# One region of 64x64 products per quad in a window-attention training kernel

## The chip, the cores and the metric

The kernel runs on one core of a Trainium2 chip. The metric is the device time of one execution in microseconds (us); the median of three timed runs stands below. A core has a matrix engine (TensorE, PE in the views; its weight loads are listed apart as PEld), a vector engine (VectorE, DVE), a scalar engine (ScalarE, ACT), GpSimd (POOL) and SyncE (SP), each with an instruction queue of its own that it works through in order, and 16 DMA engines that move data. SP and POOL issue this kernel's transfers. TensorE writes its results to PSUM, which has 8 banks; a bank holds 128 x 512 numbers in f32, and VectorE or ScalarE copy ("evict") results from there to SBUF.

## The reference

Attention inside windows of 8 x 8 pixels over a 256 x 256 image with 384 channels, one head, in bf16, and all its gradients:

```python
def forward(x, wqkv, wo):            # x: 1 x 256 x 256 x 384
    xw = windows(x)                  # 1024 windows of 64 pixels x 384
    qkv = xw @ wqkv
    q, k, v = qkv[..., :C], qkv[..., C:2 * C], qkv[..., 2 * C:]
    p = softmax(einsum('bqc,bkc->bqk', q, k) * C ** -0.5)
    return unwindows(einsum('bqk,bkc->bqc', p, v) @ wo)

out, vjp = jax.vjp(forward, x, wqkv, wo)
return (out, *vjp(grad_out))         # out, dx, dwqkv, dwo
```

## The kernel before

**Algebra.** The kernel multiplies the weights together once. With A = scale Wq Wk^T and B = Wv Wo, a window's scores are x A x^T, its output is P (x B), and the gradients need `y` (x with A), `z` (grad_out with B^T), `u` = x B and `v` (x with A^T). dS is the gradient of the scores. dx is the sum P^T z + dS^T y + dS v. The weight gradients come from two 384 x 384 sums over all pixels, x^T U and x^T W with U = dS x and W = P^T grad_out, kept in `GF_acc` and multiplied out at the end.

**Tiles.** Two windows lie on the 128 partitions, one on the lower 64 (`LO`), one on the upper (`HI`). Four such pairs make a quad; there are 128 quads. Everything that mixes channels is a full 128 x 128 product (`product`, L145). Everything inside one window is 64 x 64 and is done in `attend` (L249) by `slot`, which issues four 64 x 64 matmuls (L266) that occupy the four quarters of the array: two halves of a "straight" product and two of a "crossed" one. A call of `attend` treats two of the quad's four `t` and has six slots; a row of consecutive slots is called a region here.

**Pipeline.** `step(c, b, a, ahead)` works on three quads at once: attention of quad `c`, scores and softmax of `b`, projections of `a`, and loads for one three quads ahead. The schedule is by hand: on each engine instructions run in the order in which the Python code issues them. On TensorE one step is: `scores` of b (`sd`, 24 short products), eight `uv` evictions' products (`pj`, 384 wide), three groups of z products (`pj`, 512 wide), one group of 12 weight-gradient products (`filler(1)`, tile `pg`), the six slots of `attend(c, (0, 1))`, three groups of y products, another `pg` group, the six slots of `attend(c, (2, 3))`. A group of weight gradients sums over three quads (`GQ`), so 12 products go into one bank and VectorE adds the bank to `GF_acc` (L321).

**Evictions.** ScalarE evicts `uq` and `vq` (L235), z and y into `yz` (L159, L161), the outputs `o` (L270), most of the dx banks `pd` (L270, L296, half of the L297 copies) and one `Wq` of each pair (L281), and stacks `Pb` into `ps` (L211). VectorE evicts `Uq` (L285, L289), the other `Wq` (L283), the upper half of `pd[1]` of the first pair (L297), gathers `yz` into `zy` (L167) and does the softmax and its gradient (`soft`).

**Transfers.** SP's queue holds, in order, per step: the transposes `dT` and `xT` of a coming quad (L134), the transpose `PS<-ps` (L239), four loads of `xq` (L126), and the transpose `tok<-zy` (L171) that turns y and z. POOL's queue holds four loads of `dq` (L127) and nine output transfers (L298 to L305).

**PSUM.** All eight banks come from one pool, `ring`. A tile takes a bank when `ring.tile` is called for it, and its first write waits until the reader of the bank's tile before has finished. `attend` takes all its eight banks at its start:

```python
pw = {t: bank("pw") for t in pair}
pu = {t0: bank("pu")}
pd = [bank("pd") for outer in (0, 1)]
po = {t0: bank("po")}
pu[t1] = bank("pu")
po[t1] = bank("po")
```

The `pd` banks collect through the whole region; `pw`, `pu` and `po` are written by one slot each.

Of the kernel before, what the change touches and what calls it, by code (L numbers as in the profile page):

```python
# [9 lines left out]
ALU = mybir.AluOpType  # L10
# [12 lines left out]
def kernel(  # L23
# [91 lines left out]
    def windows(ap, st, first, count=2):  # L115
        row, col = st["at"]
        return ap[0, row + WIN * first:row + WIN * (first + count), col:col + WIN, :]
# [68 lines left out]
    def soft(st, step):  # L186
        sd = st["sd"]
        if step == 0:
            st["mx"] = mx = sm.tile([P, QUAD], F32, tag="mx", name="mx")
            for w, h in ((0, HI), (1, LO)):  # L190
                nc.vector.tensor_reduce(out=mx[h, :], in_=sd[h, :, w, :], axis=AX.X, op=ALU.max)
        elif step == 1:
            mx = st["mx"]
            st["sh"] = sh = sm.tile([P, QUAD, WT], F32, tag="sh", name="sh")
            for w, h, o in ((0, HI, LO), (1, LO, HI)):
                nc.vector.tensor_tensor(out=sh[o, :, :], in0=sd[h, :, w, :], in1=over_k(mx[h, :], WT),
                                        op=ALU.subtract)
        elif step == 2:
            st["ex"] = ex = sm.tile([P, QUAD, WT], F32, tag="ex", name="ex")
            nc.scalar.activation(out=ex[:], in_=st["sh"][:], func=ACT.Exp)  # L200
        elif step == 3:
            ex = st["ex"]
            rs = sm.tile([P, QUAD], F32, tag="rs")
            nc.vector.tensor_reduce(out=rs[:], in_=ex[:], axis=AX.X, op=ALU.add)
            ri = sm.tile([P, QUAD], F32, tag="ri")
            nc.vector.reciprocal(out=ri[:], in_=rs[:])
            st["Pb"] = Pb = qp.tile([P, QUAD, WT], BF16, tag="Pb", name="Pb")
            nc.vector.tensor_tensor(out=Pb[:], in0=ex[:], in1=over_k(ri[:]), op=ALU.mult)  # L208
            st["ps"] = ps = qp.tile([P, QUAD, 2, WT], BF16, tag="ps", name="ps")
            for w, h in ((0, LO), (1, HI)):  # L210
                nc.scalar.copy(out=ps[h, :, w, :], in_=Pb[h, :, :])  # L211
        elif step == 4:
            st["pr"] = pr = sm.tile([P, QUAD, WT], F32, tag="pr", name="pr")
            for w, h in ((0, LO), (1, HI)):
                nc.vector.tensor_tensor(out=pr[h, :, :], in0=sd[h, :, w, :], in1=st["Pb"][h, :, :], op=ALU.mult)
            st["D"] = D = sm.tile([P, QUAD], F32, tag="D", name="D")
            nc.vector.tensor_reduce(out=D[:], in_=pr[:], axis=AX.X, op=ALU.add)
        else:
            pd = sm.tile([P, QUAD, WT], F32, tag="pd")
            nc.vector.tensor_tensor(out=pd[:], in0=st["Pb"][:], in1=over_k(st["D"][:]), op=ALU.mult)  # L220
            ps = st["ps"]
            for w, h, o in ((0, LO, HI), (1, HI, LO)):
                nc.vector.tensor_tensor(out=ps[o, :, w, :], in0=st["pr"][h, :, :], in1=pd[h, :, :], op=ALU.subtract)
            st["dS"] = dS = qp.tile([P, QUAD, WT], BF16, tag="dS", name="dS")
            nc.vector.tensor_tensor(out=dS[:], in0=st["pr"][:], in1=pd[:], op=ALU.subtract)

    def uv(st, t, part):
        if t == 0 and part == 0:
# [20 lines left out]
    def attend(st, pair):  # L249
        if pair[0] == 0:  # L250
            st["Uq"] = grp.tile([P, QUAD, C], BF16, tag="Uq", name="Uq")
            st["Wq"] = grp.tile([P, QUAD, C], BF16, tag="Wq", name="Wq")

        def bank(name):
            return ring.tile([P, C], F32, tag="r", name=name)
# [12 lines left out]
        def keep(name, src):  # L268
            sb = ob.tile([P, C], BF16, tag=name, name=name)
            nc.scalar.copy(out=sb[:], in_=src[:])  # L270
            return sb

        t0, t1 = pair
        pw = {t: bank("pw") for t in pair}
        pu = {t0: bank("pu")}
        pd = [bank("pd") for outer in (0, 1)]
        po = {t0: bank("po")}
        pu[t1] = bank("pu")
        po[t1] = bank("po")
        slot((pw[t0], "Pb", "dq", t0), ("Pb", "z", t0), start=True)  # L280
        nc.scalar.copy(out=st["Wq"][:, t0, :], in_=pw[t0][:])  # L281
        slot((pw[t1], "Pb", "dq", t1), ("dS", "y", t0))
        nc.vector.tensor_copy(out=st["Wq"][:, t1, :], in_=pw[t1][:])  # L283
        slot((pu[t0], "ST", "xq", t0), ("Pb", "z", t1), start=True)
        nc.vector.tensor_copy(out=st["Uq"][:, t0, :], in_=pu[t0][:])  # L285
        slot((po[t0], "PT", "uq", t0), ("dS", "y", t1))
        o0 = keep("o", po[t0])
        slot((pu[t1], "ST", "xq", t1), ("ST", "vq", t0), stop=True)
        nc.vector.tensor_copy(out=st["Uq"][:, t1, :], in_=pu[t1][:])  # L289
        slot((po[t1], "PT", "uq", t1), ("ST", "vq", t1), stop=True)  # L290
        o1 = keep("o", po[t1])
        inner = keep("d", pd[0])
        if t0 == 0:
            st["mid"], st["rim"] = [ob.tile([P, C], BF16, tag="d", name="d") for k in range(2)]
# [6 lines left out]
        if t0 == 0:  # L301
            nc.gpsimd.dma_start(out=windows(out_1, st, 0, 1), in_=st["rim"][HI, :])
        else:
            nc.gpsimd.dma_start(out=windows(out_1, st, 3), in_=st["mid"][:])
            nc.gpsimd.dma_start(out=windows(out_1, st, 7, 1), in_=st["rim"][LO, :])  # L305

    fill = []

    final = {}

    def gf_group(sts, last=False):
        n = len(sts) * QUAD
        for f in range(2):
            if last:
                final[f] = grp.tile([P, CK, C], BF16, tag="Uq", name="GFb")
            for ma in range(CK):
                pw = ring.tile([P, C], F32, tag="r", name="pg")
                for i in range(n):
                    st, t = sts[i // QUAD], i % QUAD
                    product(pw[:], st["xq"][:, t, ma * P:(ma + 1) * P], st["UW"[f] + "q"][:, t, :], i == 0, i == n - 1)  # L320
                nc.vector.tensor_tensor(out=GF_acc[:, f, ma, :], in0=pw[:], in1=GF_acc[:, f, ma, :], op=ALU.add)  # L321
                if last:
                    nc.vector.tensor_copy(out=final[f][:, ma, :], in_=GF_acc[:, f, ma, :])
                yield

    def filler(n):
        while n and fill:
            try:
                next(fill[0])
                n -= 1  # L330
            except StopIteration:
                fill.pop(0)

    def step(c, b, a, ahead):


        def on(st):
            return (lambda f, *r: f(st, *r)) if st is not None else (lambda f, *r: None)
        C_, B, A = on(c), on(b), on(a)
        B(scores)  # L340
        B(soft, 0)
        if b is not None and c is None:
            weight_rest()
        B(uv, 0, 0)
        B(uv, 0, 1)
        B(soft, 1)
        B(uv, 1, 0)
        B(uv, 1, 1)
        B(soft, 2)
        B(soft, 3)  # L350
        B(uv, 2, 0)
        B(uv, 2, 1)
        B(uv, 3, 0)
        B(uv, 3, 1)
        B(soft, 4)
        for mo in range(CK):
            A(project, 0, mo)
        B(soft, 5)
        B(turn)
        if ahead is not None:  # L360
            load(ahead)
        filler(1)
        C_(attend, (0, 1))
        A(gather, 0)
        for mo in range(CK):
            A(project, 1, mo)
        A(gather, 1)
        A(to_tokens)
        filler(1)
        C_(attend, (2, 3))  # L370

    G_ON_PE, X_ON_PE = 4, 1
    EV = {"z": "AAA", "y": "AAA", "u": "AAAA", "v": "AAAA", "o": "AAAA", "U": "DDDD", "W": "DDDD", "d": "AAAA"}
    quads = [(row, col) for row in range(0, H, 2 * WIN * QUAD) for col in range(0, W, WIN)]
    sts = [{"at": q, "i": i} for i, q in enumerate(quads)]
    n = len(sts)
# [41 lines left out]
    with tc.manual_schedule(engines=MANUAL):  # L418
# [19 lines left out]
        for i in range(-1, n + 1):  # L438
            if 0 <= i < n - 2:
                load_turn(sts[i + 2])  # L440
            step(get(i - 1), get(i), get(i + 1), get(i + AHEAD) if i >= 0 else None)
            if 0 < i + 2 < G_ON_PE:
                turn_on_pe(sts[i + 2], "dq", "dT")
            if i == 1:
                turn_blocks(woT_sb, wo_sb)
            if i > 0:
                held.append(sts[i - 1])
                sts[i - 1] = None
            if held and i == n:
                last = gf_group(held, True)  # L450
            elif len(held) == GQ:
                fill.append(gf_group(held))
                held = []
        filler(1 << 30)
        weight_gradients(last)


# [28 lines left out]
```

## Time and profile before

| | |
|---|---|
| timed runs | 1947.11, 1947.42, 1947.66 us; median 1947.42 |
| the profiled execution | span 1942.8 us, 48771 instructions |
| granted TensorE clock | 0.999 |
| busy time in one quad (1009.30 to 1024.09, 14.79 us) | PE 14.79, PEld 8.29, DVE 11.24, ACT 11.96, POOL 6.96 us |
| full products, mean of one | `pg` and 384-wide `pj` 326 ns, 512-wide `pj` 381 ns |
| 64x64 products, mean of one | 323 to 335 ns |
| the adds to `GF_acc` (L321) | 258, mean 558 ns |
| TensorE's waits for DMA (PE rows) | `dT` 5.1 us in 4 waits, `PS` 1.5 us in 3 |
| DMA | 423.21 MB, mean 218 GB/s; the engines' mean busy share is 0.9 or more in nearly all of 40 slices |
| issue to landing, median | `tok` 7.6, `xT` 6.3, `dT` 5.9, `PS` 4.7 us |

The profiled execution is one run; its span leaves out about 4.6 us of what a timed run has. Matmuls are pipelined: a matmul's duration is its latency, and the distance between the starts of two neighbours is what it costs. A wait is shown as idle time before an instruction with what ended it. A bank tells nothing by itself in the profile; which reader frees which bank is read from the built program's order.

### The profile page before, as it was taken

The page shows a single profiled execution, that of the slowest core. Times are in us where ns is not written, and L with a number is a line of the kernel's source. Part 1 is how long each engine was busy: PE and PEld are TensorE (multiplying, and loading weights), DVE is VectorE, ACT ScalarE, POOL GpSimd, SP SyncE. Part 2 cuts the span into 40 slices and gives each one's busy share as a digit, 9 for nine tenths or more (in the row PEclk, how much of TensorE's full clock was granted, in tenths as well). Part 3 has the DMA queues.
Part 4 walks back from the last instruction along what each step waited for, and adds up shares of the span by engine and source line. Part 5 has one row for each costly group of instructions (what it writes and reads, how often), then busy time and mean ns, then how long its engine had stood idle before and what let it go on. Part 6 is the DMA issues. An engine that isn't in the chain of part 4 may idle for free.

```text
span 1942.8 us, 48771 instructions
## 1 busy us (share of the span) xinstructions
PE 1926.6 (99%) x17859; PEld 1076.9 (55%) x17859; DVE 1458.9 (75%) x3244; ACT 1546.3 (80%) x3613; POOL 895.2 (46%) x1670
## 2 busy tenths in 40 slices
PE   9999999999999999999999999999999999999999
PEld 5555555555555555555555555555555555555555
DVE  6777767777777777777777777777777777777776
ACT  7878878778777878887787878788887878887775
POOL 3445444444444445444444454454444445444432
PEclk9999999999999999999999999999999999999999
DMA  8999999999999999999999999999999999999994
GB/s 186 220 222 227 224 204 222 224 217 224 223 221 226 226 220 223 226 221 220 219 228 222 221 219 229 221 225 217 230 218 228 224 219 220 226 224 219 222 195 109
DMA packets 1017584, 423.21 MB, mean 218 GB/s; under 512 B 899584, under 2 KB 992768, under 8 KB 1017344
## 3 DMA queue, kind: packets, MB, share of 16 engines
q1 hardware_dynamic: 935984, 267.85, 79.0%
q0 software_dynamic: 79872, 151.17, 30.8%
q8 instruction: 140, 2.29, 0.5%
q10 hardware_dynamic: 1488, 1.08, 0.2%
q14 instruction: 100, 0.82, 0.1%
HBM read 101.84 MB, written 101.84 MB: 105 GB/s over the span
## 4 chain that ended last, share of the span: by engine, by line
PE 94%; ACT 2%; DMA 2%; DVE 1%; issue 0%; SPq 0%; POOL 0%; ACTq 0%; POOLq 0%
PE pj L145 49%; PE pg L145 25%; PE pw L266 6%; PE sd L145 5%; PE pu L266 4%; PE po L266 4%; DMA PS<-ps 1%; DMA dT<-dq 1%; PE pd L266 1%; ACT uq L235 0%; ACT vq L235 0%; DMA dq<-in_grad_out_dram 0%; ACT yz L159 0%; PE pe L385 0%; SPq L134 0%
## 5 line engine op out<-in xcount | busy, mean ns | idle before, releaser
L298 POOL DMA_DIRECT2D out_dram<-o x256 | 137.7, 538 | 936.8 <-ACT o L270 915.8
L145 PEld LDWEIGHTS <-xq 128*128 128x128 bf16 x3072 | 300.0, 98 | 226.4 <-issue 2.0
L145 PEld LDWEIGHTS <-xT 128*128 128x128 bf16 x3072 | 291.6, 98 | 182.7
L145 PE MATMUL pj<-B_sb,xT 128*128 128x384 bf16 x1536 | 333.5, 326 | 0.0
L145 PE MATMUL pj<-AT_sb,xT 128*128 128x384 bf16 x1536 | 333.3, 326 | 0.0
L127 POOL DMA_DIRECT2D dq<-in_grad_out_dram x512 | 271.9, 547 | 40.4 <-DMA out_dram<-o 17.6
L281 ACT CAST Wq<-pw 128x384 bf16<-128x384 f32 x256 | 123.0, 480 | 200.1 <-PE pw L266 200.0
L145 PE MATMUL pj<-dT,BT_sb 128*128 128x512 bf16 x1152 | 271.3, 381 | 5.1 <-DMA dT<-dq 5.1
L145 PE MATMUL pg<-Uq,xq 128*128 128x384 bf16 x1536 | 270.4, 326 | 0.5 <-DVE GF_acc L321 0.5
L145 PE MATMUL pj<-xT,A_sb 128*128 128x512 bf16 x1152 | 270.8, 380 | 0.0
L145 PE MATMUL pg<-Wq,xq 128*128 128x384 bf16 x1536 | 270.4, 326 | 0.0
L321 DVE TENSOR_TENSOR GF_acc<-pg,GF_acc 128x384 f32<-128x384 f32 x258 | 143.9, 558 | 152.8 <-PE pg L145 152.7
L235 ACT CAST uq<-pj 128x384 bf16<-128x384 f32 x512 | 249.9, 488 | 7.3 <-PE pj L145 1.0
L235 ACT CAST vq<-pj 128x384 bf16<-128x384 f32 x512 | 255.1, 498 | 0.1
L270 ACT CAST o<-po 128x384 bf16<-128x384 f32 x512 | 220.9, 484 | 5.1 <-PE po L266 2.4
L211 ACT COPY ps<-Pb 64x256 bf16<-64x256 bf16 x256 | 103.2, 403 | 149.7 <-DVE Pb L208 148.2
L159 ACT CAST yz<-pj 128x512 bf16<-128x512 f32 x384 | 206.7, 644 | 2.1 <-PE pj L145 2.0
L161 ACT CAST yz<-pj 128x512 bf16<-128x512 f32 x384 | 200.8, 607 | 0.2
L145 PEld LDWEIGHTS <-BT_sb 128*128 128x128 bf16 x1152 | 112.4, 98 | 129.8 <-DMA dT<-dq 7.0
L145 PEld LDWEIGHTS <-A_sb 128*128 128x128 bf16 x1152 | 102.3, 98 | 139.9 <-issue 33.6
L167 DVE COPY zy<-yz 128x1536 bf16<-128x1536 bf16 x256 | 143.4, 560 | 46.3 <-ACT yz L161 39.8
L266 PE MATMUL pd<-tok,Pb 64*64 64x384 bf16 x1024 | 173.3, 335 | 0.0
(89 smaller groups left out, 3376.1 us busy)
## 6 DMA issues: line engine op xcount, KB each, us to landing
xq<-in_x_dram SPq DMA_DIRECT2D x512, 96.0 KB, 4.2
dq<-in_grad_out_dram POOLq DMA_DIRECT2D x512, 96.0 KB, 4.0
out_dram<-o POOLq DMA_DIRECT2D x512, 96.0 KB, 4.0
out_dram<-d POOLq DMA_DIRECT2D x384, 96.0 KB, 4.2
out_dram<-d POOLq DMA_DIRECT2D x256, 48.0 KB, 4.3
tok<-zy SPq DMA_TRANSPOSE x128, 7.6
PS<-ps SPq DMA_TRANSPOSE x128, 4.7
xT<-xq SPq DMA_TRANSPOSE x127, 6.3
```

The source lines that it names most:

```text
L127: nc.gpsimd.dma_start(out=dq[:, t, :], in_=windows(grad_out, st, 2 * t))
L145: nc.tensor.matmul(out, lhsT=lhsT, rhs=rhs, start=start, stop=stop)
L159: ENG[EV["z"][mo]](out=yz[:, mo, :, 0:4:3, :], in_=pj[:])
L161: ENG[EV["y"][mo]](out=yz[:, mo, :, 1:3, :], in_=pj[:])
L167: nc.vector.tensor_copy(out=st["zy"][:, kind, :, :, :, :], in_=src)
L211: nc.scalar.copy(out=ps[h, :, w, :], in_=Pb[h, :, :])
L235: cp(out=dst[:, t, :], in_=pj[:])
L266: nc.tensor.matmul(dst, lhsT=operand(st, lhs, t, h), rhs=operand(st, rhs, t, h), **flags)
L270: nc.scalar.copy(out=sb[:], in_=src[:])
L281: nc.scalar.copy(out=st["Wq"][:, t0, :], in_=pw[t0][:])
L298: nc.gpsimd.dma_start(out=windows(out_0, st, 2 * t0), in_=o0[:])
L321: nc.vector.tensor_tensor(out=GF_acc[:, f, ma, :], in0=pw[:], in1=GF_acc[:, f, ma, :], op=ALU.add)
```

## The change

*One region.* `attend` becomes a generator that yields after each of its six slots. The weight-gradient groups become generators too (`gf_slots`): each full product is replaced by four 64 x 64 products in the same pattern as a slot, into two banks (`straight` and `crossed`), which VectorE adds to `GF_acc` one after the other. `attention_and_gradients` deals 24 such slots (two groups of 12) and the 12 attention slots of a quad out in the order of the string `SLOTS`. The groups of full products remain for the last quads (`gf_rows`, `gf_final`).

*y products ahead.* The first gather and the three groups of y products are issued before the region. The second gather and the transpose `tok` are issued after the sixth attention slot (`GATHER_AT`).

*Banks at first write.* `pw`, `pu` and `po` take their bank just ahead of the slot that writes it.

*Smaller edits.* The copies of `Pb` into `ps` (now `stack`) are issued on ScalarE two `uv` evictions later. The `Wq` copy of the last `t` moves from VectorE to ScalarE.

```diff
+    def stack(st):
+        for w, h in ((0, LO), (1, HI)):
+            nc.scalar.copy(out=st["ps"][h, :, w, :], in_=st["Pb"][h, :, :])
...
-        pw = {t: bank("pw") for t in pair}
-        pu = {t0: bank("pu")}
+        pw = bank("pw")
         pd = [bank("pd") for outer in (0, 1)]
-        po = {t0: bank("po")}
-        pu[t1] = bank("pu")
-        po[t1] = bank("po")
-        slot((pw[t0], "Pb", "dq", t0), ("Pb", "z", t0), start=True)
-        nc.scalar.copy(out=st["Wq"][:, t0, :], in_=pw[t0][:])
-        slot((pw[t1], "Pb", "dq", t1), ("dS", "y", t0))
-        nc.vector.tensor_copy(out=st["Wq"][:, t1, :], in_=pw[t1][:])
+        slot((pw, "Pb", "dq", t0), ("Pb", "z", t0), start=True)
+        nc.scalar.copy(out=st["Wq"][:, t0, :], in_=pw[:])
+        yield
+        pw = bank("pw")
+        slot((pw, "Pb", "dq", t1), ("dS", "y", t0))
+        copies[EV["W"][t1]](out=st["Wq"][:, t1, :], in_=pw[:])
+        yield
...
+    def gf_slots(sts, f, ma):
+        straight, crossed = [ring.tile([P, C], F32, tag="r", name="pg") for k in range(2)]
+        n = len(sts) * QUAD
+        for i in range(n):
+            st, t = sts[i // QUAD], i % QUAD
+            for h in (LO, HI):
+                products = ((h, straight), (OTHER[h.start], crossed))
+                for o, dst in products if h == LO else products[::-1]:
+                    nc.tensor.matmul(dst[o, :], lhsT=st["xq"][h, t, ma * P + o.start:ma * P + o.stop],
+                                     rhs=st["UW"[f] + "q"][h, t, :], start=(i == 0), stop=(i == n - 1))
+            if i == n - 1:
+                gf_add(f, ma, [straight, crossed])
+            yield
...
+    def attention_and_gradients(st):
+        pairs = (slot for pair in ((0, 1), (2, 3)) for slot in attend(st, pair))
+        groups = (slot for k in range(min(2, len(fill))) for slot in gf_slots(*fill.pop(0)))
+        seen = 0
+        for kind in SLOTS:
+            next(pairs if kind == "a" else groups, None)
+            seen += kind == "a"
+            if kind == "a" and seen == GATHER_AT:
+                yield
...
         B(uv, 2, 1)
+        B(stack)
         B(uv, 3, 0)
...
-        filler(1)
-        C_(attend, (0, 1))
         A(gather, 0)
         for mo in range(CK):
             A(project, 1, mo)
+        region = attention_and_gradients(c) if c is not None else iter(())
+        next(region, None)
         A(gather, 1)
         A(to_tokens)
-        filler(1)
-        C_(attend, (2, 3))
-
+        for rest in region:
+            pass
+
+    SLOTS, GATHER_AT = "ggagggagggagaagggaggggggaggaagagagag", 6
-    EV = {..., "W": "DDDD", ...}
+    EV = {..., "W": "ADAA", ...}
```

## The prediction

> **What bounds the kernel now.** I read the busy times and the chain first, then one quad on TensorE, then the evictions behind an attention region, then SP's queue.
>
> ```profile
> PE 1926.6 (99%) x17859; PEld 1076.9 (55%) x17859; DVE 1458.9 (75%) x3244; ACT 1546.3 (80%) x3613; POOL 895.2 (46%) x1670
> ...
> PE 94%; ACT 2%; DMA 2%; DVE 1%; issue 0%; SPq 0%; POOL 0%; ACTq 0%; POOLq 0%
> ```
>
> TensorE is the chain. So a change pays through TensorE's time per quad, and costs through whatever makes TensorE wait. The next view is TensorE's instructions in order of time (start, duration).
>
> ```profile
> 1006.15 2.12 PE L145 MATMUL pg<-Wq,xq 128*128 128x384 bf16 x12
> 1008.19 0.35 PE L266 MATMUL pw<-dq,Pb 64*64 64x384 bf16 x1
> ...
> 1008.38 0.33 PE L266 MATMUL pd<-tok,dS 64*64 64x384 bf16 x2
> ...
> 1008.54 0.32 PE L266 MATMUL pu<-xq,PS 64*64 64x384 bf16 x1
> ...
> 1009.03 0.32 PE L266 MATMUL po<-uq,PS 64*64 64x384 bf16 x1
> ...
> 1009.30 0.87 PE L145 MATMUL sd<-xT,yz 128*128 128x64 bf16 x24
> ...
> 1024.09 0.88 PE L145 MATMUL sd<-xT,yz 128*128 128x64 bf16 x24
> ```
>
> A quad lasts 14.79 to 14.80 us (`sd` to `sd`; 14.795 below). Over the 256 attention regions of the trace the median slot starts are 0, 187, 349, 512, 674 and 837 ns: a slot of four 64x64 products takes 163 ns once under way. A full product `pg` takes 162.5 ns. At a region's edges time is lost: last `pg` to first slot 256 ns where 162.5 would do (+93), first slot 187 (+24), last slot to the next full product 264 (+101), that product 228 instead of 215.5 (+12). Together 0.230 us a region, two regions a quad.
>
> The third view is ScalarE and VectorE behind the region that starts at 1017.89, whose last slot starts at 1018.73.
>
> ```profile
> 1018.79 0.86 ACT L270 CAST o<-po 128x384 bf16<-128x384 f32 x2
> ...
> 1019.53 0.50 ACT L270 CAST d<-pd 128x384 bf16<-128x384 f32 x1
> ...
> 1019.90 0.48 ACT L296 CAST d<-pd 64x384 bf16<-64x384 f32 x1
> ...
> 1020.42 0.56 DVE L297 CAST d<-pd 64x384 bf16<-64x384 f32 x1 [0.47 <-ACT d L296]
> ...
> 1021.01 0.56 DVE L167 COPY zy<-yz 128x1536 bf16<-128x1536 bf16 x1
> ```
>
> The reader should see one chain: `o`, `d`, the lower half of `pd[1]`, and only then VectorE's upper half (L297), which ends 2.25 us after the last slot began. Today nothing on TensorE needs that bank so soon.
>
> The last view is SP's queue.
>
> ```profile
> 1014.97 4.68 SPq L171 DMA_TRANSPOSE tok<-zy  x1
> 1019.88 1.44 SPq L134 DMA_TRANSPOSE dT<-dq  x1
> 1021.50 2.94 SPq L134 DMA_TRANSPOSE xT<-xq  x1
> 1024.60 1.50 SPq L239 DMA_TRANSPOSE PS<-ps  x1
> 1026.15 3.29 SPq L126 DMA_DIRECT2D xq<-in_x_dram  x4
> 1029.56 4.74 SPq L171 DMA_TRANSPOSE tok<-zy  x1
> ```
>
> It never rests: four kinds of transfer fill the whole quad, and it runs 6 to 8 us behind what it could start. TensorE waits for it seldom: over the trace `dT` landed late in 3 quads (3.1 us), `PS` in 4 (4.6 us).
>
> **The change, part by part.** *One region less.* 24 slots at 163 in place of 24 products at 162.5: +0.012 us. One pair of edges less: -0.230. Net -0.218 us a quad, 14.577 if nothing waits.
>
> *Instruction count.* Each of 24 products becomes four loads and four matmuls; a region has 144 pairs in 36 x 163 ns = 5.87 us, 41 ns a pair. The trace shows 24 slot pairs in 1.10 us followed by 24 `sd` pairs in 0.71, 38 ns a pair, over 48 pairs only. I take nothing; the dear end is a rival below.
>
> ```profile
> L145 PEld LDWEIGHTS <-xq 128*128 128x128 bf16 x3072 | 300.0, 98 | 226.4 <-issue 2.0
> ...
> L266 PEld LDWEIGHTS <-PS 64*64 64x64 bf16 x3072 | 129.6, 106 | 51.8 <-DMA PS<-ps 3.5 <-issue 3.3
> ```
>
> These are the weight loads: mean 98 ns for a full block, 106 for a quarter. Four quarters one after another would be 424 ns a slot; at a 163 ns pitch they overlap. The Trainium skill, TensorEngine Tiling (Array Packing), Restrictions, says that column tiling rules out fast weight load, which speaks against moving full products to 64x64; unhidden, its cost here would be 24 x (0.424 - 0.163) = 6.3 us a quad, but the slots already in the kernel show it hidden.
>
> *Banks at first write.* In the built program each bank's first write waits for one named reader. I number the 36 slots; attention's are 3, 7, 11, 13, 14, 18 and 25, 28, 29, 31, 33, 35. Time zero is the start of slot 18 (`po` of the first pair). Durations and distances are those of the third view and of equal rows.
> Slot 18's result starts its copy 0.385 after the slot's start, as the first `o` of a region does now (ScalarE is free: it ends the y evictions about 1.9 us earlier). Then `d` 0.755, lower half 1.125 to 1.61, VectorE's upper half at 1.643 to 2.203 (today's 2.252 less the 0.049 that `o` queued behind another `o`). TensorE follows a VectorE end by 0.055 (first quads of the trace). Slot 31 is due at 13 x 0.1627 = 2.115 and its `po` takes exactly this bank: it waits until 2.258, +0.143.
> VectorE goes on: second gather at 1.643 + 0.592 (distance L297 to L167), `Uq` of slot 29 another 0.592 later, 0.548 long, end 3.375. The next quad's `sd` takes that bank: earliest 3.43. Without this wait `sd` would start at 18 x 0.1627 + 0.143 + 0.26 = 3.335, so +0.095.
> What else waits for VectorE there: `Uq` of slot 33 (3.84; needed by the second `vq` product 1.2 after `sd`), two gradient adds, then the softmax, whose first step starts 1.5 after `sd` instead of 0.98; its last result is still 6 us ahead of its use. Bounds: the second wait vanishes if the `Uq` copy follows the gather at 0.464, as copies follow each other (-12 us over 123 quads); slot 32 after a wait may come at 187 instead of 163 (+3 us). I take the rows as measured.
>
> *Other edits.* Two more adds a quad (0.558 each) and one `Wq` copy (0.548) moved from VectorE to ScalarE: VectorE 11.25 + 1.12 - 0.55 = 11.8 of 14.8 us. The adds of the first group end 0.27 before VectorE's upper half is ready to start, so the chain above hides them; later by more, they would lengthen both waits. The moved `Wq` sits behind the lower half on ScalarE and in no wait. The ScalarE copies of `Pb` (0.82) go behind two evictions and use the 1.16 us in which ScalarE idled; nothing: TensorE waits for no eviction there today, and if a bank did come late by all of it, 0.82 us a quad.
>
> *y products ahead.* Same nine products. Their `xT` is now needed 6.55 us after `sd`, not 9.9: of 119 landings 9 would be late, 8.9 us in all. The y evictions now stand on ScalarE ahead of the region's and end before them. The second gather ends 0.6 us before the next `sd`, not 1.7, but SP takes `tok` some 6 us after it and does not feel it. `PS` is needed 1.4 us later: 4.6 us of lateness becomes 0.8. With `dT` unchanged that is 3.1 + 4.6 before, 3.1 + 8.9 + 0.8 after, partly in the same quads: +0 to +5, I take +1. POOL's output and `dq` transfers, two bursts a quad (1009.9 to 1014.9, 1019.6 to 1021.8), close up to nearly one; SP's delays come from them, and the trace has no such row. Bounds: -8 (all such waits gone), or SP later by 1 us, where lateness on `xT` grows to 21 us (+12).
>
> **Sum.** -0.230 + 0.012 + 0.143 + 0.095 = +0.020 us a quad, x 123 quads = +2.5; +1 for DMA. The profiled execution spans 1942.8, so 1946.3; the timed runs have 1947.42, 4.6 above the span: 1951.
>
> **Rivals.** *Covers hold* (faster): the two waits don't occur, because the gather or the upper half comes earlier than the rows say. Then 1947.4 - 0.218 x 123 + 1 = 1922. For it: both waits are short beside chains of 2.2 and 3.4 us, 6% off decides. Against: the distances repeat within 2 ns from quad to quad.
> *SP falls behind* (slower): `tok` to `xq` together take 13.9 us plus 0.66 of gaps out of 14.8, and POOL's burst lies differently. It decides once SP's mean period passes TensorE's 14.81. SP 2 us later makes `xT` late by 42 us in all instead of 8.9: 1951 + 33 = 1984. Against: when SP was over 8 us behind, it took only 14.5 us a quad and caught up.
> *Issue of instructions* (slower): if pairs can't be issued at 41 ns beyond 48 in a row; at 50 ns the region takes 7.2, +1.33 us a quad, less the two waits, which then hide: about 1947 + 123 x 1.1 = 2080. No row shows a run that long.
> The Trainium skill, TensorE: Matmul & The Clock Gate, Back-to-back issue gap, gives a floor of some 25 ns a matmul, or 62 where its sequencer decodes in software; by the first it is hidden, by the second 144 x 62 ns = 8.9 us, an estimate near 2325 us. Only a longer run can tell.
> *It doesn't do what it says*: the edge cost is per change of product shape, and a slot order with banks in between might keep it. Then 1951 + 28 = 1979; against it, the slots inside a region show none.
>
> **How the numbers follow.** Waits eat the gain 0.56 (spread 1938 to 1962, on both sides of no change), covers hold 0.14, SP behind 0.17, issue 0.07, edges stay 0.06. Likeliest 1951. A measurement of this kernel tells about 0.2% (3.9 us) from no change. From the first case 0.12 faster, 0.24 same, 0.20 slower; the covers add 0.14 faster, the other three 0.30 slower, of which 0.03 may vanish into same: faster 0.26, same 0.27, slower 0.47. The range takes the first case with its bounds and half of SP's: 1937 to 1972.
>
> **What would show it.** Right: one region of about 5.9 us a quad; `po` of slot 31 waiting some 0.14 us for VectorE's upper half of `pd[1]` and `sd` some 0.1 for `Uq`; period near 14.8. Wrong: a period of 14.58 (no waits), slots at over 170 ns (issue), or many TensorE waits on `xT` or `dT`.

## The result and the profile after

| | before | after |
|---|---|---|
| timed runs, us | 1944.04 to 1947.66, median 1947.26 (4) | 1984.85, 1989.42, 2003.43, 2009.57, median 1996.43 |
| profiled execution, span, us | 1942.8 | 1983.1 |
| a quad in which TensorE waits for no transfer, us | 14.795 | 14.80 |
| TensorE beyond that in quads 5 to 123, us | 6.2 | 44.6 |

The ratio is 1.0265 [1.0214, 1.0316]: slower, and 45 us over the 1951 forecast, outside the range. The forecast rival "SP falls behind" gave 1984. Ratios here leave disturbed runs out, so where a kernel's times scatter, its ratio and the quotient of its medians differ.

The head of the page and its chain of waits, after:

```profile
PE 1930.0 (97%) x26859; PEld 1173.6 (59%) x26859; DVE 1556.4 (78%) x3366; ACT 1642.5 (83%) x3741; POOL 893.5 (45%) x1670
...
PE 76%; DMA 17%; issue 2%; ACT 2%; POOL 1%; DVE 1%; SPq 0%; ACTq 0%; POOLq 0%
PE pj L145 36%; PE pg L341 23%; DMA xT<-xq 15%; PE po L269 4%; PE sd L145 4%; PE pw L269 4%; PE pu L269 3%; PE pd L269 1%; DMA out_dram<-d 1%; DMA dq<-in_grad_out_dram 1%; PE pg L145 1%; DMA dT<-dq 1%; POOL dq L127 0%; SPq L134 0%; ACT uq L237 0%
```

TensorE held 94% of the chain before. Now 17% of it is DMA, and nearly all of that is one transfer, `xT`. The list of waits (us in total, times, longest) names the same one; these are all of TensorE's waits for `xT` and `dT`:

```profile
PEld L145 <- DMA xT<-xq: 58.2, 52, 3.4
...
PE pj L145 <- DMA xT<-xq: 32.6, 31, 2.9
...
PEld L145 <- DMA dT<-dq: 7.3, 7, 3.5
...
PE pj L145 <- DMA dT<-dq: 4.8, 4, 3.1
```

TensorE did not wait for `xT` once before. (A weight load and the product behind it can both be counted, so the lines do not add up to the 44.6.)

TensorE at the end of a region in order of time:

```profile
1115.42 0.33 PE L341 MATMUL pg<-Wq,xq 64*64 64x384 bf16 x4
1115.73 0.32 PE L269 MATMUL po<-uq,PS 64*64 64x384 bf16 x1
...
1115.89 0.36 PE L341 MATMUL pg<-Wq,xq 64*64 64x384 bf16 x4
...
1116.54 0.36 PE L341 MATMUL pg<-Wq,xq 64*64 64x384 bf16 x4
1116.91 0.36 PE L145 MATMUL sd<-xT,yz 128*128 128x64 bf16 x7
```

and VectorE beside it:

```profile
1115.12 0.56 DVE L306 CAST d<-pd 64x384 bf16<-64x384 f32 x1 [0.27 <-ACT d L305]
1115.71 0.56 DVE L167 COPY zy<-yz 128x1536 bf16<-128x1536 bf16 x1
1116.30 0.56 DVE L288 CAST Uq<-pu 128x384 bf16<-128x384 f32 x1
```

The slot of `po` comes 0.31 us after its neighbour where 0.16 is usual, and 0.05 after the upper half of `pd[1]` (L306) ends; `sd` comes 0.05 after `Uq` (L288) ends. These are the two bank waits of the forecast.

SP's queue over one quad:

```profile
1100.14 3.35 SPq L134 DMA_TRANSPOSE xT<-xq  x1
1103.65 1.69 SPq L241 DMA_TRANSPOSE PS<-ps  x1
1105.40 3.30 SPq L126 DMA_DIRECT2D xq<-in_x_dram  x4
1108.81 4.72 SPq L171 DMA_TRANSPOSE tok<-zy  x1
1113.75 1.53 SPq L134 DMA_TRANSPOSE dT<-dq  x1
1115.45 3.17 SPq L134 DMA_TRANSPOSE xT<-xq  x1
```

`xT` to `xT` takes 15.31 us here, and SP goes from one transfer to the next within 0.25 us; TensorE's quad takes 14.80.

### The profile page after: what moved, and what is told of

The parts are those of the page before. It is cut to its first block, busy times and chain, and to the rows that moved or that the text cites. A ratio compares the mean times of both kernels' runs of the same rounds, so it can differ in the third digit from the quotient of the medians.

```text
span 1983.1 us, 67148 instructions
## 1 busy us (share of the span) xinstructions
PE 1930.0 (97%) x26859; PEld 1173.6 (59%) x26859; DVE 1556.4 (78%) x3366; ACT 1642.5 (83%) x3741; POOL 893.5 (45%) x1670
## 3 DMA queue, kind: packets, MB, share of 16 engines
q1 hardware_dynamic: 935984, 267.85, 81.1%
q0 software_dynamic: 79872, 151.17, 30.7%
## 4 chain that ended last, share of the span: by engine, by line
PE 76%; DMA 17%; issue 2%; ACT 2%; POOL 1%; DVE 1%; SPq 0%; ACTq 0%; POOLq 0%
PE pj L145 36%; PE pg L341 23%; DMA xT<-xq 15%; PE po L269 4%; PE sd L145 4%; PE pw L269 4%; PE pu L269 3%; PE pd L269 1%; DMA out_dram<-d 1%; DMA dq<-in_grad_out_dram 1%; PE pg L145 1%; DMA dT<-dq 1%; POOL dq L127 0%; SPq L134 0%; ACT uq L237 0%
## 5 line engine op out<-in xcount | busy, mean ns | idle before, releaser
L341 PEld LDWEIGHTS <-xq 64*64 64x64 bf16 x12000 | 355.4, 107 | 158.9 <-issue 53.0
L273 ACT CAST o<-po 128x384 bf16<-128x384 f32 x512 | 244.7, 480 | 214.8 <-PE po L269 213.5
L341 PE MATMUL pg<-Wq,xq 64*64 64x384 bf16 x5952 | 361.6, 323 | 0.0
L341 PE MATMUL pg<-Uq,xq 64*64 64x384 bf16 x6048 | 360.1, 324 | 0.1
L323 DVE TENSOR_TENSOR GF_acc<-pg,GF_acc 128x384 f32<-128x384 f32 x508 | 282.1, 555 | 13.4 <-PE pg L145 4.8
L237 ACT CAST uq<-pj 128x384 bf16<-128x384 f32 x512 | 243.8, 476 | 10.3 <-PE pj L145 4.1
L161 ACT CAST yz<-pj 128x512 bf16<-128x512 f32 x384 | 212.7, 639 | 24.1 <-PE pj L145 19.6
L284 DVE CAST Wq<-pw 128x384 bf16<-128x384 f32 x128 | 71.4, 558 | 203.3 <-PE pw L269 203.2
L159 ACT CAST yz<-pj 128x512 bf16<-128x512 f32 x384 | 203.4, 618 | 2.2 <-PE pj L145 2.0
L269 PE MATMUL po<-uq,PS 64*64 64x384 bf16 x1024 | 177.2, 325 | 1.7 <-ACT Wq L280 0.8
L269 PE MATMUL pu<-xq,PS 64*64 64x384 bf16 x1024 | 174.1, 323 | 0.0
L269 PE MATMUL pw<-dq,Pb 64*64 64x384 bf16 x1024 | 171.0, 323 | 0.1
```

The lines of the kernel that those rows point to most:

```text
L159: ENG[EV["z"][mo]](out=yz[:, mo, :, 0:4:3, :], in_=pj[:])
L161: ENG[EV["y"][mo]](out=yz[:, mo, :, 1:3, :], in_=pj[:])
L237: cp(out=dst[:, t, :], in_=pj[:])
L269: nc.tensor.matmul(dst, lhsT=operand(st, lhs, t, h), rhs=operand(st, rhs, t, h), **flags)
L284: copies[EV["W"][t1]](out=st["Wq"][:, t1, :], in_=pw[:])
L341: nc.tensor.matmul(dst[o, :], lhsT=st["xq"][h, t, ma * P + o.start:ma * P + o.stop], rhs=st["UW"[f] + "q"][h, t, :], start=(i == 0), stop= ...
```

## The experiments

The expectations use letters. L: SP's pace is enough, `xT` is only needed some 3 us sooner. P: SP's queue itself has become slower than 14.80 a quad, because POOL's transfers lie differently. G: the 64x64 gradient products cost it. Two came later. N: only `xT`'s margin counts. Q: what counts is on which of SP's transfers POOL's fall. "SP's period" below is the mean distance between the starts of successive `PS` transposes over 110 quads of the profile; "quad" is TensorE's, where it waits for no transfer.

| run | time, us | ratio | quad | SP's period |
|---|---|---|---|---|
| e2_y_between | 1950.45 | 1.0050 [1.0025, 1.0074] | 14.80 | 14.94 |
| e3_before_y_ahead | 1994.71 | 1.0263 [1.0234, 1.0291] | 15.15 | 15.29 |
| e11_y_ahead_held | 1979.37 | 1.0183 [1.0166, 1.0200] | 15.15 | 15.16 |
| e7_no_out | 1934.67 | 0.9953 [0.9934, 0.9972] | 14.80 | 14.78 |
| e7b_no_wait_no_out | 1906.52 | 0.9810 [0.9795, 0.9824] | 14.57 | 14.57 |
| e5_dq_held | 1954.82 | 1.0049 [1.0032, 1.0066] | 14.80 | 14.93 |
| e12_turns_lead | 1994.35 | 1.0272 [1.0249, 1.0295] | 14.80 | 15.32 |
| e14_before_joined | 2012.59 | 1.0361 [1.0321, 1.0401] | 14.80 | 15.46 |
| e13_outs_joined | 2067.60 | 1.0627 [1.0564, 1.0689] | 14.80 | 15.97 |
| e8_no_wait_held | 1957.81 | 1.0057 [1.0027, 1.0087] | 14.57 | 14.91 |
| e15_no_wait_lead | 1996.95 | 1.0277 [1.0251, 1.0304] | 14.57 | 15.33 |
| e9_xq_on_pool | 2106.30 | 1.0824 [1.0723, 1.0926] | 14.57 | 16.11 |
| before, after | 1947.26, 1996.43 | 1.0265 [1.0214, 1.0316] | 14.80, 14.80 | 14.86, 15.21 |

SP's period alone does not say who sets the pace. The two engines wait for each other, so over 110 quads SP's period comes close to TensorE's mean quad, waits included (14.85 before, 15.18 after). What tells is whether SP rests. In every run of this table but four, the gaps between its transfers come to 0.89 us a quad, before the change too; they are longer in e7 (1.48), e7b (2.96), e11 (1.50) and e9 (1.13). In e7, e7b and e11 `tok` goes out 0.03 us (median) after `zy` is written; before it stood 6.9 us in the queue, after 7.9. So before the change, too, SP was always behind and worked without a pause.

### Which part of the change costs it

**e2_y_between.** The changed kernel with the y products back between two regions.

```diff
+        region = attention_and_gradients(c) if c is not None else iter(())
+        next(region, None)
         A(gather, 0)
         for mo in range(CK):
             A(project, 1, mo)
-        region = attention_and_gradients(c) if c is not None else iter(())
-        next(region, None)
         A(gather, 1)
```

> The changed kernel with the first gather and the y products put back between the sixth and the seventh attention slot, so there are two regions a quad again, each with 12 gradient slots. L: xT has 3 us more, the waits for it go; 14.58 plus one pair of edges 0.23 is 14.81: 1945 to 1957. P: POOL's outputs of the two pairs are some 2 us further apart again, so SP's pace recovers: the same. Theory G (the 64x64 gradient slots themselves slow the DMA or TensorE, by their instruction loads or their doubled adds): 1975 or more.

1950.45: the 24 gradient slots are still there and the loss is gone, so G falls. L and P both allow it.

**e3_before_y_ahead and e11_y_ahead_held.** The kernel before with the y products ahead of the first group; then the same with the `dq` loads held (the hold is shown below).

```diff
-        filler(1)
-        C_(attend, (0, 1))
         A(gather, 0)
         for mo in range(CK):
             A(project, 1, mo)
+        filler(1)
+        C_(attend, (0, 1))
         A(gather, 1)
```

> The kernel before with one edit: the first gather and the y products ahead of the first gradient group. L: xT is needed earlier by the first gradient group and region (3.1 us); by the landings of the trace of before 9 quads are late by 8.9 us, so 1950 to 1960. P: the two pairs' outputs close up here too (one gradient group and one region between them), so SP slows: 1970 to 1990. G: 1945 to 1952.

> The kernel before with the first gather and the y products ahead of the first filler and attend (1994.71 alone), and the dq loads held by POOL until dS of the quad is written, as in the run that brought the changed kernel to 1954.8. P: the same lever brings this one back too, SP's mean period from 15.30 to 14.9-15.0, 1948-1962. L: xT is needed as early as without the hold, 1985-2000. Q: between, 1950-1990.

1994.71 looked as if the y order alone made the whole loss. That reading fell with e11, which stayed at 1979.37 though TensorE waits for no transfer there beyond the first quads. From e11's list of waits:

```profile
PEld L269 <- issue: 136.8, 401, 0.5
...
PE po L269 <- DVE GF_acc L324: 20.0, 123, 0.2
```

A quad of e11 takes 15.15 us, undisturbed: `po` now waits 0.16 us in 123 quads for a bank that an add to `GF_acc` frees, and there are 401 pauses before quarter loads where the kernel before has 272. That `po` slot starts 0.33 us later than it did before, and so it does in e3. That is 0.35 x 123 = 43 us on TensorE, a cost the changed kernel does not have. So most of e3's loss tells nothing of the changed kernel, and no expectation foresaw the bank. The remaining 15 us between e3 and e11 do speak for P: SP does not rest in e3, at 15.29, and rests in e11.

### What the two bank waits cost

**e7_no_out and e7b_no_wait_no_out.** The changed kernel without the outputs of the first 120 quads, then the same with another order of the slots.

```diff
         (nc.scalar.copy if t0 else nc.vector.tensor_copy)(out=upper[HI, :], in_=pd[1][HI, :])
+        if st["i"] < 120:
+            yield
+            return
         nc.gpsimd.dma_start(out=windows(out_0, st, 2 * t0), in_=o0[:])
...
-    SLOTS, GATHER_AT = "ggagggagggagaagggaggggggaggaagagagag", 6
+    SLOTS, GATHER_AT = "ggagggagggagaagggaggggggggaggaagagaa", 12
```

> The changed kernel without the output transfers (out and dx) of the first 120 quads; all arithmetic stays. That takes two thirds of POOL's traffic away. P: SP runs freely, no wait for DMA is left, and what remains is TensorE's own period, 14.81 with the two bank waits: 1938 to 1947. L: the same, if xT then lands 3 us sooner; if waits for xT stay, neither holds.

> The changed kernel without the output transfers of the first 120 quads, and with another order of the slots in which neither of the two bank waits is left. The run without these transfers and with the changed kernel's own order of slots took 1934.7, all quads at 14.80. If the two bank waits cost 0.238 us a quad as predicted, a quad takes 14.57-14.58 and the run 1905-1910; if their cost is mostly taken up elsewhere, 1920-1934.

1934.67 and 1906.52. With two thirds of POOL's traffic gone no transfer is late and SP rests. The distances in the two traces: slot 31 starts 303 ns after slot 30 with the waits, 163 without; `sd` starts 372 ns after the last slot with them, 265 without. The quads take 14.796 and 14.566: the waits cost 0.230 us a quad, 28 us in all. Without them the change would be worth 14.795 - 14.566 = 0.229 us a quad.

### What makes `xT` late

**e5_dq_held.** The changed kernel with a small copy ahead of POOL's `dq` loads, so that they go out when `dS` is written, some 5 us later in the quad. Nothing else is edited.

```diff
+        if hold is not None:
+            held_by = sm.tile([P, QUAD, WT], BF16, tag="held", name="held")
+            nc.gpsimd.tensor_copy(out=held_by[:, 0, :], in_=hold["dS"][:, 0, :])
         for t in range(QUAD):
             nc.sync.dma_start(out=xq[:, t, :], in_=windows(x, st, 2 * t))
             nc.gpsimd.dma_start(out=dq[:, t, :], in_=windows(grad_out, st, 2 * t))
...
-            load(ahead)
+            load(ahead, b)
```

> The changed kernel with POOL's four dq loads held back until dS of the step is written (some 8 us after sd) by a small copy on POOL that reads it; so POOL's transfers fall into two bursts again. L: SP's place in time doesn't change, 1980 to 2005. P: SP's mean period falls back under 15.0 and most waits for xT go: 1950 to 1970.

1954.82. SP's work, its order and what TensorE needs when are the same, and 42 us of the loss are gone: SP's period falls from 15.21 to 14.93, `xT` lands 2.6 us sooner (median), and what TensorE waits beyond 14.80 falls from 44.6 to 17.0 us.

**e1_tok_later and e6_turns_first.** SP's order changed: `tok` behind the next quad's `xT`; then `dT`, `xT`, `xq`, `tok`, `PS`.

```diff
-        A(to_tokens)
...
             if 0 <= i < n - 2:
                 load_turn(sts[i + 2])
+            if i >= 0 and get(i + AHEAD) is not None:
+                load(get(i + AHEAD))
+            if 0 <= i < n:
+                to_tokens(sts[i])
...
```

(e6; e1 is without the second `if`, and its loads stay in `step`.)

> The changed kernel with SP's queue reordered: tok is issued behind the next step's dT and xT, so both stand some 4.5 us earlier in the queue. Nothing else moves. Theory L (late only: SP's pace is enough, xT is merely needed 3.3 us sooner than in the old order): TensorE's waits for xT and dT go, a quad takes 14.80, 1950 us (1943 to 1958). Theory P (pace: SP's queue itself takes some 15.1 to 15.2 us a quad now, whatever the order within it): 1975 to 2005, waits as before.

> The changed kernel with SP's queue in the order dT, xT, xq, tok, PS: dT and xT stand some 4.5 us earlier against the quad than before, and tok and PS lie between the loads of xq and the transpose that needs them (in the first try of this, e1, xT had to wait for xq just issued). L (late only): the waits for xT go and nothing else comes late: 1943 to 1958. P (pace: SP needs some 15.1 us a quad): the queue falls behind further until the next transfer is late, tok or PS: 1975 to 2005.

2116.79 (1.0914 [1.0854, 1.0974]) and 2063.46 (1.0615 [1.0587, 1.0643]), beyond every theory. In e1 the transposes stand right behind the loads they read, so the gaps in SP's queue come to 2.15 us a quad instead of 0.89, and `tok` becomes late; in e6 `tok` does. Two changes at once: neither run tells L from P.

**e10_before_closed, then e14_before_joined and e13_outs_joined.** The four outputs of a quad's first pair are to go out with the five of the second. e10 only moved their issue in the program; POOL has nothing in between, so it sent them when it did before, and nothing changed.

> The kernel before with one edit: the four output transfers of an attend's first pair are issued by POOL with the five of the second pair, so that POOL's nine outputs and four dq loads make one stretch of some 7 us instead of 2.3 and 5.1. PE's and SP's order stay as they were. P (the stretch slows SP's queue): SP's mean period rises from 14.91 to 15.1-15.2, 1970-2000 us. L (only lateness against need counts; neither xT nor tok is needed sooner here): 1943-1955. A third reading, Q: what counts is which of SP's instructions POOL's transfers fall on; here dT and xT, which had the first pair's outputs beside them, are freed, and tok gets some: 1935-1955.

1942.56 (1.0001 [0.9986, 1.0017]): no test, but it shows how well a time repeats. In e14 (the kernel before) and e13 (the changed one) POOL really waits:

```diff
+        if t0 == 0:
+            st["first"] = o0, o1, inner
+            return
...
+        held_by = sm.tile([P, WT], BF16, tag="held", name="held")
+        nc.gpsimd.tensor_copy(out=held_by[:], in_=o0[:, 0:WT])
```

(and then the nine output transfers of both pairs)

> The kernel before with the same hold: the first pair's four outputs go out with the second pair's five. Q: SP's lag falls by some us, but xT wasn't late here, so 1935-1945. P in its first form: 1960-1990. N: 1938-1950.

> The changed kernel with the first pair's four output transfers held on POOL until the second pair's first row is written, so that all nine lie in one stretch of about 5 us, the dq loads behind it. Q (place): POOL's transfers no longer lie on dT and xT, SP's lag falls and xT lands 1 us or more sooner: 1945-1965. P in its first form (a longer stretch slows SP): 1985-2010. N alone: within 10 us of 1996.

2012.59 and 2067.60. The edits change only when POOL sends: in e14 the four outputs go some 5 us later, and behind them the other five by 2.3 and the `dq` loads by 3.1. No byte and no place in SP's queue changes, yet SP's period goes from 14.86 to 15.46 and from 15.21 to 15.97. N and Q fall. P in its first form has the direction right, though both times lie above its ranges. Page part 6 (median from issue to landing, us) shows most of it in one transfer; e13, then after, which it is made of:

```profile
tok<-zy SPq DMA_TRANSPOSE x128, 10.1
```

```profile
tok<-zy SPq DMA_TRANSPOSE x128, 7.3
```

(8.9 in e14, 7.6 before.) In e13 the nine outputs and the `dq` loads lie just ahead of `tok` and on its start.

**e12_turns_lead.** The changed kernel with `xT` transposed a whole quad sooner (`load_turn` takes the quad of `dT` and that of `xT`; a fourth `xT` buffer, `xq` loaded a quad sooner, fewer `dq` and output buffers to make room).

```diff
-            if 0 <= i < n - 2:
-                load_turn(sts[i + 2])
+            if 0 <= i:
+                load_turn(get(i + 2), get(i + 3))
```

> The changed kernel with xT transposed one quad further ahead (xq loaded one quad further ahead, a fourth xT buffer; dq 5 buffers instead of 6, output rows 6 instead of 8, to make room). SP's order and POOL's stay. N (only xT's margin): no xT is late any more, quads of 14.80, 1935-1945. P (SP's queue can't keep 14.80): its lag grows until PS, tok or dT is late, 1960-1985.

1994.35, as before the edit. No wait for `xT` is left in the list; these have taken its place:

```profile
PEld L148 <- DMA dT<-dq: 41.7, 40, 3.4
...
PEld L272 <- DMA PS<-ps: 33.9, 40, 2.1
...
PE pu L272 <- DMA PS<-ps: 20.1, 25, 1.7
PE pj L148 <- DMA dT<-dq: 17.5, 20, 3.1
```

This decides against L and N. It is not one transfer with too little margin: SP's queue takes over 15 us for a quad without a rest, and the wait moves to other transfers. (The buffers taken away are part of this edit; no run has them alone.)

### A version that beats both?

**e8_no_wait_held, e9_xq_on_pool, e15_no_wait_lead**, all with e7b's slots, so 14.57 us a quad on TensorE, and with all outputs. e8 holds `dq` as e5 does, e15 has e12's lead, e9 gives SP's `xq` loads to POOL:

```diff
-            nc.sync.dma_start(out=xq[:, t, :], in_=windows(x, st, 2 * t))
+            nc.gpsimd.dma_start(out=xq[:, t, :], in_=windows(x, st, 2 * t))
```

> The dq loads held back as in e5, and the slots dealt out so that the two bank waits go (the seventh attention slot two places later, the second gather at the end of the region): TensorE's own period 14.58. P: SP's pace, 14.9 in e5, is now the bound: 1940 to 1960, with more time in waits for DMA than in e5. L: the 0.24 us a quad come off in full: 1915 to 1930.

> The order of slots without the two bank waits (14.57 us a quad, 1906.5 without outputs) with all outputs, the dq loads not held, and xT transposed one quad further ahead. N: xT no longer late, 1906-1925, faster than the kernel before. P: SP's queue keeps some 14.9 a quad whatever the margin, 1945-1960.

> Slots as in e8, dq not held, but the four loads of xq issued by POOL instead of SP, which takes 2.8 us a quad off SP's queue and adds as many bytes to POOL's. P, if SP's own issuing counts: SP under 14.5 a quad, waits mostly gone: 1918 to 1940. P, if only the bytes of POOL's bursts count: 1970 or more.

1957.81, 1996.95 and 2106.30. TensorE's 0.23 us a quad bring nothing once SP sets the pace: e8 is no faster than e5, e15 no faster than e12. e9 takes 2.8 us of issue a quad off SP, and SP's period still grows to 16.11; the landing times of e9 show where the time goes:

```profile
tok<-zy SPq DMA_TRANSPOSE x128, 11.9
PS<-ps SPq DMA_TRANSPOSE x128, 7.8
xT<-xq SPq DMA_TRANSPOSE x127, 9.8
```

All are far above the changed kernel (7.3, 5.7, 7.5) and the kernel before (7.6, 4.7, 6.3). What SP's transposes take depends on what POOL has in flight. e8 and e9 lie where P put them (e9 by its second reading); e15 lies 37 us above P's range, as e12 lay 9 us above it.

**e16_no_wait_spread and e17_spread.** The `dq` loads held until `D`, 1.6 us earlier than `dS`, so that POOL's gaps are about equal; with e7b's slots and with the changed kernel's own.

```diff
+            held_by = sm.tile([P, QUAD], F32, tag="held", name="held")
+            nc.gpsimd.tensor_copy(out=held_by[:], in_=hold["D"][:])
```

> The order of slots without the two bank waits (14.57 us a quad on TensorE), with the dq loads held by POOL until D is written (about 1.8 us earlier than dS, in the middle between the second pair's outputs and the next first pair's): POOL's gaps are about 3 us each. If an even spread is what SP needs: SP's mean period 14.6-14.75, 1910-1935. If the run with dS as the hold (1957.8, SP 14.95) already has all that spreading can give: 1950-1960.

> The changed kernel with its own order of slots (14.80 on TensorE) and the dq loads held until D is written. If an even spread is what SP needs: SP keeps up, no DMA waits, 1934-1942. If not: as with dS as the hold, 1950-1958.

e16 took 1938.85 to 2008.75, median 1976.01 (12 runs; 1.0050 [1.0016, 1.0085]); e17 1933.41 to 1973.23, median 1952.78 (7 runs; 1.0008 [0.9972, 1.0045]). Neither beats the kernel before; no version with all outputs did. An even spread is not enough by itself: three of e17's runs lie at 1933 to 1938, as expected if it were, and four at 1953 to 1973. The executions traced took 1969.4 (e17) and 1974.0 us (e16); in them SP does not rest, at 15.05 and 15.20. What sets the shorter executions apart no trace shows.

## Why the prediction was wrong

**Right: the terms on TensorE.** One region less, without waits: 14.577 predicted, 14.566 measured. `po` of slot 31: +143 ns predicted, +142 (305 less 163; 303 in e7_no_out). `sd`: +95 predicted, +107. All together 14.815 predicted, 14.80 measured. The chain behind each wait is the one that was worked out. The gain of the region was given back to the two waits almost exactly, as forecast.

**Right: issue and edges.** 36 slots in a row keep 162.5 ns, 144 pairs at 41 ns. The first rule weighed, from the Trainium skill, TensorEngine Tiling (Array Packing), Restrictions, that column tiling rules out fast weight load, costs nothing visible here: the pitch of `pg` slots equals that of attention's. The second, from the skill's TensorE: Matmul & The Clock Gate, Back-to-back issue gap, had a dear branch of 62 ns a matmul; the region at 41 ns a pair of load and matmul excludes it for this run.

**Wrong: the DMA term, "I take +1".** It should have been 44.6 - 6.2 = +38. With it the forecast's own sum gives 1942.8 + 2.5 + 38.4 = 1983.7, against a span of 1983.1 (one execution). Three steps of it failed.

*"9 would be late, 8.9 us in all."* This laid the need of the new order over the landings of the old trace. The need was right: 6.55 us after `sd`. (That of the old order was 9.70, not 9.9; at neither was a landing late.) But `xT` now lands 0.58 us ahead of it (median) where the old landings gave 2.54, so 42 of 119 are late, 39.5 us. The forecast's own row for "SP 2 us later" gave 42 us; it stood in the rival, not in the sum.

*"13.9 us plus 0.66 of gaps out of 14.8."* This gave SP some 0.2 us to spare in each quad. Over 110 quads of the same trace the transfers take 13.96 and the gaps 0.89, together the period of 14.86: nothing to spare. The rival's own condition, a period above 14.81, was met before the change. (The 0.05 us over 14.81 in 118 quads is the 6.2 us that TensorE waited.)

*"When SP was over 8 us behind, it took only 14.5 us a quad and caught up."* This is what the rival was turned down with, and it is a reading of picked quads. Where the lag neither grows nor shrinks over the run, quads picked for a long lag must on average be followed by a shorter one, whatever the pace. In the changed kernel too, SP takes 15.3 to 15.45 at 8.5 to 10 us behind but 14.80 at over 10 (33 quads). The mean is what counts, and e5, e13 and e14 show that it goes with where POOL's transfers lie. The forecast saw that these "close up to nearly one" and that no row showed it, and then bounded their effect at 1 us of lateness (+12). A change of pace has no such bound: SP's lag grows in every quad until TensorE waits, so 0.35 us a quad is paid 123 times (43 us).

**The rival "SP falls behind"** named the mechanism, the point from which it decides (14.81; SP's period is 15.21) and 1984 (the profiled execution: 1984.85). Its chance of 0.17 was too small. That its 1984 comes so close is luck: the 2 us were picked as an example, not derived, and `xT`'s margin fell by 1.96. The timed median lies 12 us above the profiled execution, and no trace shows those other runs.

**What stays open** is the rule by which the place of POOL's transfers sets SP's pace. What differs most plainly is the longest pause in POOL's queue; here it is in one quad of before, then of after (idle time in brackets):

```profile
1012.79 2.13 POOL L127 DMA_DIRECT2D dq<-in_grad_out_dram  x4
1019.56 0.54 POOL L298 DMA_DIRECT2D out_dram<-o  x1 [4.64 <-ACT o L270]
```

```profile
1106.52 0.52 POOL L127 DMA_DIRECT2D dq<-in_grad_out_dram  x1 [0.29 <-DMA out_dram<-o]
1113.82 0.54 POOL L307 DMA_DIRECT2D out_dram<-o  x1 [6.78 <-ACT o L273]
```

When POOL issues, as a mean over the quads, in us after `sd`, against SP's period:

| | outputs, 1st pair | outputs, 2nd pair | `dq` | SP's period |
|---|---|---|---|---|
| before | 10.3 to 12.7 | 0.6 to 3.4 | 3.4 to 5.7 | 14.86 |
| e5_dq_held | 11.8 to 14.6 | 0.2 to 3.8 | 8.7 to 10.8 | 14.93 |
| after | 12.1 to 14.9 | 0.5 to 3.2 | 3.5 to 6.2 | 15.21 |
| e14_before_joined | 0.6 to 6.1, both pairs | | 6.4 to 8.9 | 15.46 |
| e13_outs_joined | 0.1 to 5.6, both pairs | | 5.9 to 8.4 | 15.97 |

In these five rows a longer period goes with a longer pause in which POOL issues nothing (the longest of a quad, as a mean: 4.5, 5.0, 5.9, 7.1, 7.4 us). It is no rule: in the executions traced, e16 and e17 have 3.8 us, with periods of 15.20 and 15.05, and e5's three groups stand almost as close together as those of after. Whether SP's own phase matters is not shown: that in the kernel before it took 15.8 us a quad when 6.5 to 7.3 us behind and 14.5 at over 8 is again a reading of picked quads.

## What to carry to other kernels

A transfer that is in time with little margin is no constant: before its need is moved, ask what sets its landing, and treat a queue that never rests as a rate to be compared with the period, as a mean over the run, not as a lateness to be added. Moving computation by a microsecond or two also moves the outputs behind it on another queue, and the two queues share the DMA engines. An experiment that repeats one part of a change in the old kernel must be looked at in its trace before its time is read: the same 1.026 had for the most part another cause there.

## What was not expected of the hardware

While POOL's queue had 12 or more packets in flight (20% of the time in the kernel before), SP's had 2.0 on average; with POOL's queue empty (41%), 19.4. The changed kernel gives 1.7 (23%) and 19.3 (47%). By page part 3 of the trace after, POOL's packets hold 1.9 KB on average (151.17 MB in 79872), SP's 286 bytes (267.85 MB in 935984). The Trainium skill, DMA: Bandwidth & Descriptors, Queues, rings and completion order, says that a DMA engine takes turns between queues a packet at a time; the rows agree with that in kind. But nothing here shows that the profile counts the same packets as that sentence, and no run changed their size, so it is not shown to be the cause.

An SP transpose's time on SP is not fixed either: `PS` took from 1.19 us up, 1.48 on average before and 1.93 after; `xT` 2.99 and 3.24, from 1.43 up. And moving POOL's transfers, four outputs by some 5 us and the rest of a quad's by 2 to 3, with no byte more, cost the kernel before 3.6%.
